# H3 convolution beside a ReLU feed-forward block: new pacing weights for the convolution's steps, and another preparation of the first two token blocks

## The chip, the cores and the metric

The kernel runs on one core of a Trainium2 chip. Its time is the device time of one execution in microseconds (us); three runs of the kernel before took 1110.46, 1113.22 and 1113.85 us, so their median is 1113.22 us. Engines are named TensorE (PE in the rows of the profile; its weight loads are PEld), VectorE (DVE), ScalarE (ACT), GpSimd (POOL) and SyncE (SP, which here only issues DMAs).

## The reference

For 2048 tokens of 576 numbers, with a hidden width of 4608:

```python
x = A_q
xn = _layernorm(x, axis=-1)                      # (x - mean) / sqrt(var + 1e-5)
return x + _A_ref(xn, A_k, A_v, A_shift_k, A_ssm_k, A_ssm_D) + _B_ref(xn, B_w1, B_w2)

# _B_ref: the feed-forward block
h = jnp.maximum(xn @ w1, 0); return h @ w2       # 576 -> 4608 -> 576

# _A_ref: k through a causal convolution of 4 taps, times v, then a causal
# convolution as long as the sequence (FFT of length 4096), a skip term, times q
k_shift = sum(k_pad[:, t:t + S] * shift_k[:, ks - 1 - t] for t in range(4))
kv = k_shift * v
y = irfft(rfft(kv, 4096) * rfft(ssm_k, 4096))[:2048] + kv * ssm_D
return q * y                                     # q is xn
```

## The kernel before, in words

**Two programs in one.** TensorE works through the feed-forward block, and the steps of the convolution are slipped in between. The 2048 tokens are four blocks of 512. A half (two blocks) is taken through all 18 groups of 256 hidden columns, then the other half; one group for one half is called a quad here, so there are 36 quads, numbered `g`. `classical` forms hidden sums with plain products in quads 0 and 1 (`PLAIN = 2`). From quad 2 on `quad` forms the two blocks' hidden sums with seven products instead of eight, on operands that are parts of the transposed tokens ("00", "01", "11") and their sums and differences ("s1" to "s4"). Every operand is held as a rounded part and the rest of it (`hi`, `lo`), so that one product of a 128-row chunk is three matmuls of 512 columns. `hidden` (L511) turns a finished PSUM bank into the operands of the second layer: ScalarE writes `hh`, then VectorE writes `ll` (L516). Two PSUM banks (pool `ps_h`) hold the hidden sums, so TensorE can start a new sum in a bank only when that bank's `ll` has been written. The second layer takes 12 matmuls of 288 columns for 128 tokens (`mm2`, tile `pso`, two tiles of two banks), which VectorE adds to `acc` (L652, L648); such a unit of 128 tokens is done eight times a quad. GpSimd forms the low parts of the weights (L439) and issues their DMAs.

**The first stage** (L1019 to L1078, pool `fa`) gets the half's operands ready. `first_xT` subtracts the mean from the tokens of block 0, transposes them on TensorE (tiles `psx`, `psf`), and splits the result; VectorE and ScalarE share the centring. The factor 1/std is left to the sums: `mm2` multiplies by `rstd` for block 0. For block 1 `second_rows` waits for statistics of all eight tiles, normalizes in full on ScalarE, and `second_xT` transposes through the two `psf` banks. From quad 1's classical sums on, `whole` puts the operands of both blocks together again from their two parts (GpSimd), `scales` makes a row of 1/std with one matmul of a diagonal matrix, `scaled` multiplies block 0 by it, and `combine`/`split_operand` make "s1" to "s4".

**The convolution** is a generator, `conv`, whose stages are: fb (`later_operands`: the second half's tokens are normalized, written to memory, read back transposed and split), fk (the filter's first transform, tiles `ks`, `wk`), fx (taps, gate, split and first transform of k and v; VectorE lines L772, L775, L776, L781 and L672; matmuls `psf<-xs,wx`), fm (the middle transforms) and fo (the way out). In fm, `spectrum` is a turn of 8 matmuls from `ztk` into two banks `psf`, copied out by four ScalarE copies (L856); `product_of` is a turn of 8 from `ztx` into the next two `psf`, multiplied out by VectorE (L871); `way_back` is a turn of 16. The pool `ps_f` has two banks in all, so each turn needs both banks of the turn before it to be read out. The matmuls of fm and fo stand in the program's order among those of the feed-forward block (`in_turn`).

**What paces it.** After each group of feed-forward matmuls `tick` adds their columns to a clock. When the convolution's clock allows, the next piece of `conv` is written into the program. A piece costs the weight that it yields (`W_FB`, `W_FK`, `W_FX`, `W_FMK`, `W_FMX`, `W_FMB`, `W_FO`); `rate` is the sum of all weights (`FFT_TOTAL`) over the columns of the feed-forward block (`SHARE` of them, less `PAUSES` times 16000 for the pauses). So only the ratios of the weights matter: they say how many feed-forward columns lie beside each stage. `here()` keeps a piece's VectorE and ScalarE instructions behind the last `acc` and the last `hh` at that place; within that, a scheduler places instructions.

Of the kernel before, what the change touches and what calls it, by code (L numbers as in the profile page):

```python
# [50 lines left out]
PAUSES = 18  # L51
SHARE = 0.993
# [53 lines left out]
def h3_ffn_kernel(ctx: ExitStack, tc, x, k, v, shift_k, ssm_k, ssm_D, w1, w2, fwd, inv, mid, out):  # L106
# [86 lines left out]
    lows = []  # L193

# [52 lines left out]
    def first_xT(pool):  # L247

        xn = rows_tiles(pool, 0)
        wide = [ps_o.tile([P, 2, 512], F32, tag="o", name=f"psx{k}") for k in range(2)]  # L250
        ps = [wide[c // 2][:, c % 2, :] for c in range(4)] + [fft_psum()]
        last = {}
        for t in range(BT):
            last[t] = centre(xn[t], acc[t], t, ("dve", "act")[t % 2], last.get(t - 2))
            transposes(ps, xn[t], t)
            keep_warm(WARM_TILE[t])
        for o in ("00", "01"):
            operand(o)
        rest_operand(0)
        with tc.issue_after(last[BT - 1].ins):  # L260
            split_a(0)
            for c in range(4):
                split_chunk(xo["00" if c < 2 else "01"], c % 2, ps[c])
            high, done["low"] = split_rest(hl[0], ps[4])
        with tc.issue_after(high.ins):
            split_r(0)
            split_b(0)
            split_d(0)
            xf["r"] = pool.tile([64, 512], F32, tag="xfr", name="xfr")
            nc.scalar.activation(xf["r"], ps[4][:64], AF.Copy)  # L270
        with tc.issue_after(done["low"].ins):
            for t in (1, 3):
                stats(t, acc[t])

    def second_rows(pool):
        xn = rows_tiles(pool, 1)
        for o in ("10", "11"):
            operand(o, "s4" if o == "10" else None)
        rest_operand(1)
        for t in range(BT, 2 * BT):  # L280
            with tc.issue_after(lows[(t - BT) // 2].ins):
                stats(t, acc[t])
        with tc.issue_after(lows[1].ins):
            last = inv_std(0, 2 * BT)
        neg = xp.tile([P, BT], F32, tag="negs", name="negs")
        with tc.issue_after(last.ins):
            nc.vector.scalar_tensor_tensor(neg, mv[:, BT:2 * BT, 0], -1.0, rstd[:, BT:2 * BT],
                                           op0=OP.mult, op1=OP.mult)
        for i in range(BT):
            t = BT + i  # L290
            nc.scalar.activation(xn[i], acc[t], AF.Identity, bias=neg[:, i:i + 1],
                                 scale=rstd[:, t:t + 1])
        return xn

    def second_xT(xn):
        for c in range(5):
            w = min(P, D - c * P)
            ps = fft_psum()
            for i in range(BT):
                nc.tensor.transpose(ps[:w, i * P:(i + 1) * P], xn[i][:, c * P:c * P + w], ident)  # L300
            if c == 4:
                split_rest(hl[1], ps)
            else:
                split_chunk(xo["10" if c < 2 else "11"], c % 2, ps)

    def whole(pool, o):

        xf[o] = pool.tile([P, 2, 512], F32, tag=f"xf{o}", name=f"xf{o}")
# [4 lines left out]
    def scales(pool):  # L313

        diag = pool.tile([P, BT, P], F32, tag="diag", name="diag")
# [798 lines left out]
```

## Time and profile before

| | |
|---|---|
| Median of three runs | 1113.22 us (1110.46 to 1113.85) |
| The profiled execution | 1111.22 us, of which its span is 1109.0 us |
| TensorE matmuls, busy | 1057.7 us, 95% of the span |
| VectorE, ScalarE, GpSimd, busy | 766.8, 478.0, 470.1 us |
| Mean granted TensorE clock | 0.981 |

Rows of the profile read: start in us from the span's begin, length in us, engine, line, operation, out<-in, shapes, count; in brackets the engine's idle time before it and what ended it. Matmuls overlap (a row's length of one is longer than the distance to the next), so a busy TensorE can still be late: pace is read from distances between starts. The stages of the profiled execution lie at about 0 to 80 us (first stage), 80 to 140 (first part of fb), 140 to 260 (rest of fb and loads), 260 to 410 (fk), 410 to 680 (fx), 690 to 970 (fm), 970 to 1109 (fo and the end).

### The profile page before, as it was taken

The page shows a single profiled execution, that of the slowest core. Times are in us where ns is not written, and L with a number is a line of the kernel's source. Part 1 is how long each engine was busy: PE and PEld are TensorE (multiplying, and loading weights), DVE is VectorE, ACT ScalarE, POOL GpSimd, SP SyncE. Part 2 cuts the span into 40 slices and gives each one's busy share as a digit, 9 for nine tenths or more (in the row PEclk, how much of TensorE's full clock was granted, in tenths as well). Part 3 has the DMA queues.
Part 4 walks back from the last instruction along what each step waited for, and adds up shares of the span by engine and source line. Part 5 has one row for each costly group of instructions (what it writes and reads, how often), then busy time and mean ns, then how long its engine had stood idle before and what let it go on. Part 6 is the DMA issues. An engine that isn't in the chain of part 4 may idle for free.

```text
span 1109.0 us, 17042 instructions
## 1 busy us (share of the span) xinstructions
PE 1057.7 (95%) x6298; PEld 876.2 (79%) x6298; DVE 766.8 (69%) x1136; ACT 478.0 (43%) x914; POOL 470.1 (42%) x504
## 2 busy tenths in 40 slices
PE   6898999999999997999999898999999999999998
PEld 3687889988999986888888787866666676788877
DVE  3888787457877757999999997444554455456665
ACT  3343344235877742443544443344444444322220
POOL 4453355344444444444444443524232423254541
PEclk8999999999999998999999998999999999999999
DMA  5144854942444447459964332386556654376754
GB/s 141 35 115 141 170 198 177 205 88 76 149 139 138 138 137 175 129 181 365 271 168 131 120 118 84 132 237 187 186 174 195 198 183 136 125 235 183 209 185 118
DMA packets 118431, 179.45 MB, mean 162 GB/s; under 512 B 66381, under 2 KB 67551, under 8 KB 116556
## 3 DMA queue, kind: packets, MB, share of 16 engines
q1 hardware_dynamic: 99212, 121.99, 37.0%
q0 software_dynamic: 18816, 55.49, 16.9%
q10 hardware_dynamic: 320, 0.88, 0.3%
q8 instruction: 50, 0.82, 0.3%
q14 instruction: 33, 0.27, 0.1%
HBM read 123.27 MB, written 45.61 MB: 152 GB/s over the span
## 4 chain that ended last, share of the span: by engine, by line
PE 67%; DVE 19%; issue 5%; DMA 4%; ACT 2%; SPq 1%; POOL 1%; DVEq 0%; POOLq 0%; ACTq 0%
PE pso L495 29%; PE psh L495 26%; PE psf L690 8%; DVE e L775 4%; DVE acc L652 3%; DVE c L776 3%; DVE ll L516 2%; PE psh_c L495 2%; PE psf L678 2%; DMA r<-in_w 1%; DVE xs L672 1%; DVE c L772 1%; DVE c L781 1%; SPq L372 1%; DVE sums L451 1%
## 5 line engine op out<-in xcount | busy, mean ns | idle before, releaser
L495 PE MATMUL pso<-w,hh 128*128 128x288 f32 x2304 | 474.5, 298 | 3.2 <-DVE acc L652 1.6
L495 PEld LDWEIGHTS pso<-w,hh 128*128 128x128 f32 x2304 | 382.5, 189 | 37.1 <-issue 9.0
L495 PE MATMUL pso<-w,ll 128*128 128x288 f32 x1152 | 340.7, 296 | 0.2 <-DVE ll L516 0.2
L652 DVE TENSOR_TENSOR acc<-pso,acc 128x576 f32<-128x576 f32 x280 | 210.7, 753 | 173.7 <-PE pso L495 172.6
L495 PEld LDWEIGHTS pso<-w,ll 128*128 128x128 f32 x1152 | 218.0, 189 | 0.4 <-DVE ll L516 0.4
L439 POOL TENSOR_TENSOR w<-r,w 128x576 fp32r<-128x576 f32 x72 | 110.6, 1542 | 139.9 <-ACT w L438 139.9
L439 POOL TENSOR_TENSOR wb<-sums,wb 128x512 fp32r<-128x512 f32 x34 | 48.1, 1414 | 205.5 <-ACT wb L438 188.8
L495 PE MATMUL psh<-x,wa 128*128 128x512 f32 x408 | 110.2, 404 | 10.1 <-DVE p L607 4.9
L495 PE MATMUL psh<-xs,wb 128*128 128x512 f32 x408 | 109.4, 400 | 1.9 <-ACT u L577 1.9
L495 PEld LDWEIGHTS psh<-x,wa 128*128 128x128 f32 x408 | 74.2, 190 | 34.2 <-issue 6.9
L495 PEld LDWEIGHTS psh<-xs,wb 128*128 128x128 f32 x408 | 71.9, 188 | 26.2 <-issue 12.4
L495 PE MATMUL psh<-hl,wr 128*128 128x512 f32 x272 | 88.2, 402 | 2.1 <-ACT psh L600 2.0
L600 ACT ACTIVATE psh<-psh 128x512 f32<-128x512 f32 x34 | 19.9, 585 | 150.8 <-DVE u L598 150.8
L516 DVE SCALAR_TENSOR_TENSOR ll<-psh,hh 128x512 fp32r<-128x512 f32 x68 | 46.7, 687 | 50.5 <-ACT hh L515 50.1
L515 ACT ACTIVATE hh<-psh 128x512 fp32r<-128x512 f32 x68 | 40.6, 597 | 84.7 <-PE psh L495 84.5
L495 PE MATMUL psh<-xs,wc 128*128 128x512 f32 x204 | 59.3, 428 | 15.4 <-DVE ll L516 15.4
L439 POOL TENSOR_TENSOR wd<-r,wd 128x256 fp32r<-128x256 f32 x36 | 34.6, 961 | 89.9 <-ACT wd L438 89.8
L439 POOL TENSOR_TENSOR wa<-r,wa 128x512 fp32r<-128x512 f32 x36 | 52.3, 1452 | 40.8 <-ACT wa L438 40.5
L672 DVE TENSOR_TENSOR ks<-kt,ks 64x288 fp32r<-64x288 f32 x64 | 54.5, 852 | 18.4 <-ACT ks L671 16.9
L495 PEld LDWEIGHTS psh<-xs,wc 128*128 128x128 f32 x204 | 40.2, 202 | 29.0 <-DVE ll L516 17.6
L495 PEld LDWEIGHTS psh<-hl,wr 128*128 128x128 f32 x272 | 47.6, 189 | 15.7 <-issue 6.6
L776 DVE TENSOR_TENSOR c<-c,e 128x576 f32<-128x576 f32 x48 | 55.3, 1152 | 0.5
(152 smaller groups left out, 1610.5 us busy)
## 6 DMA issues: line engine op xcount, KB each, us to landing
r<-in_w POOLq DMA_DIRECT2D x70, 288.0 KB, 3.5
r<-in_w POOLq DMA_DIRECT2D x35, 512.0 KB, 5.3
zk<-zk SPq DMA_DIRECT2D x32, 288.0 KB, 3.0
zx<-zx SPq DMA_DIRECT2D x32, 288.0 KB, 2.6
ztk<-zk SPq DMA_DIRECT2D x18, 512.0 KB, 3.9
ztx<-zx SPq DMA_DIRECT2D x18, 512.0 KB, 4.3
k<-k SPq DMA_DIRECT2D x72, 128.0 KB, 3.7
zy<-vo SPq DMA_DIRECT2D x18, 512.0 KB, 2.7
```

The lines of the kernel that those rows point to most:

```text
L372: nc.sync.dma_start(w[32 * i:32 * i + 32].rearrange("p (g d) -> p g d", d=32), src[:, :, d:d + 32])
L439: nc.gpsimd.tensor_tensor(w[:, 1, :n], src, w[:, 0, :n], OP.subtract)
L495: last = nc.tensor.matmul(ps, a, m, start=start and n == 0, stop=n == len(seq) - 1, skip_group_check=True)
L515: done["act"] = nc.scalar.activation(hh, ps, AF.Relu)
L516: low = nc.vector.scalar_tensor_tensor(ll, ps, 0.0, hh, op0=OP.max, op1=OP.subtract)
L600: nc.scalar.activation(x, y, AF.Copy, scale=-1.0)
L652: done["acc"] = nc.vector.tensor_tensor(two(acc[t]), ps[:, :, :NH], two(acc[t]), OP.add)
L672: nc.vector.tensor_tensor(dst[other], src[own], dst[own], OP.subtract)
L678: nc.tensor.matmul(ps[:, :NH], w[:, u, n, :], stk, start=n == 0, stop=n == 1)
L690: done["pe"] = nc.tensor.matmul(ps, a, m, start=start, stop=stop)
L775: nc.vector.tensor_tensor(e, win[t - n], sk[:, n, :], OP.mult)
L776: nc.vector.tensor_tensor(sums[t], sums[t], e, OP.add)
```

## The change

**Pacing.** All weights are new, and with them `SHARE` (0.993 to 0.99), `PAUSES` (18 to 19), `N_FB` (36 to 37) and one pause ahead of fx (1.5 to 2.5 times 16000). The sum of the weights goes from 514.4 to 971.9. Worked out from the constants, and counted in the order of the program on TensorE:

| stage | sum of weights, before and now | share of the clock, in thousand columns | columns between its first and last matmul |
|---|---|---|---|
| fb | 57.6, 144.3 | 171, 223 | none on TensorE |
| fk | 96.0, 160.0 | 284, 247 | 272192, 272192 |
| fx | 166.4, 371.2 | 493, 574 | 439008, 492256 |
| fm | 122.4, 190.8 | 362, 295 | 355712, 290304 |
| fo | 72.0, 105.6 | 213, 163 | 197376, 149760 |

**The first stage.** `block_xT` now treats both blocks alike: centred only, by VectorE and ScalarE in turn, transposed through `psx` and `psf`, split, and copied whole to `xf` by ScalarE from PSUM. `second_rows`, `second_xT` and `whole` go. All eight units of quads 0 and 1 multiply by `rstd` (L652 of the new code). `scales` and `scaled` are done for both blocks, and all of "00", "01", "11" and the rest rows are made again scaled. Each piece is now held behind the last `acc` and `hh` (`here()`), so they stand in the order in which the code is written. The weights' split of quad 0's second layer comes after block 1's centring, the DMA of its weights ahead of the last two tiles of tokens, and quad 0's units after both blocks' hidden sums. Statistics of the second half are inverted four tiles at a time (before two).

```diff
-PAUSES = 18
-SHARE = 0.993
+PAUSES = 19
+SHARE = 0.99
-W_FK, W_FX, W_FMK, W_FMX, W_FMB, W_FO = 1.5, 2.6, 1.6, 3.2, 2.0, 4.5
+W_FK, W_FX, W_FMK, W_FMX, W_FMB, W_FO = 2.5, 5.8, 2.4, 4.8, 3.4, 6.6
-N_FB, W_FB = 36, 1.6
+N_FB, W_FB = 37, 3.9
+    def block_xT(pool, b, names, tags):
...
+        for t in range(BT):
+            last[t] = centre(xn[t], acc[b * BT + t], b * BT + t, ("dve", "act")[t % 2],
+                             done["copied"] if b and t == 1 else last[t - 2])
...
+            for c in range(4):
+                nc.scalar.activation(dst[c][:, 0], ps[c], AF.Copy)
+            high = nc.scalar.activation(hl[b][:64], ps[4][:64], AF.Copy)
+            for c in range(4):
+                nc.vector.tensor_tensor(dst[c][:, 1], ps[c], dst[c][:, 0], OP.subtract)
...
+            for o, src in zip(names, wide):
+                xf[o] = pool.tile([P, 2, 512], F32, tag=f"xf{o}", name=f"xf{o}")
+                nc.scalar.activation(xf[o], src, AF.Copy)
...
-    def whole(pool, o):
...
-            nc.gpsimd.tensor_tensor(xf[o][:, c, :], xo[o][:, 0, c, :].bitcast(F32),
-                                    xo[o][:, 1, c, :].bitcast(F32), OP.add)
...
-        if g < PLAIN and b == 0:
+        if g < PLAIN:
...
-            yield -1.5 * PAUSE
+            yield -2.5 * PAUSE
...
     with tc.tile_pool(name="fa", bufs=1) as fa:
-        first_xT(fa)
-        load_w1(1)
+        block_xT(fa, 0, ("00", "01"), (None, None))
         classical(0, 0, 0, 1, 1)
         classical(0, 0, 1, 0, 2)
-        xn = second_rows(fa)
+        block_xT(fa, 1, ("10", "11"), ("s4", None))
+        load_w1(1)
+        with tc.issue_after(done["low"].ins):
+            inv_std(0, 2 * BT)
         for j in range(FT):
             split_w2(0, j)
             load_w2(1, j)
-        for i in range(BT):
-            open_unit(0, 0, i)
-            mm2(0, 0, i)
-        second_xT(xn)
         classical(0, 1, 0, 1, 0)
...
+        for i in range(BT):
+            unit(0, i)
+        row = scales(fa, 0)
+        scaled(row, "00", "01", 0)
         classical(1, 0, 0, 0, 0)
-        row = scales(fa)
-        for o in ("00", "01"):
-            whole(fa, o)
         unit(1, 0)
         unit(1, 1)
...
+        row = scales(fa, 1)
+        scaled(row, "11", "10")
+        combined(fa, "s1")
+        made("s1")
         classical(1, 0, 1, 1, 0)
...
         unit(1, 2)
         unit(1, 3)
-        sums(2)
...
+        combined(fa, "s2")
+        made("00")
+        made("01")
+        made_rest(0)
+        made("s2")
         classical(1, 1, 0, 0, 0)
         split_a(2)
+        sums(2)
```

**The order at three places.** On ScalarE at the very start, before (`wa0`, `wr0`, `wb0`, `wd0` are first-layer weights, `w20` second-layer weights, `x00`, `x01`, `hl0` the operands of block 0, `psx` and `psf` the transposed tokens):

```order
L438 ACTIVATE wa0_205<-r1_0_106 128x512
L208 ACTIVATE x00_202<-psx0_155 128x512
L208 ACTIVATE x01_203<-psx1_156 128x512
L438 ACTIVATE w20_313<-r2_0_0_117 128x576
L204 ACTIVATE hl0_204<-psf_157 64x512
L438 ACTIVATE wr0_218<-r1_0_106 128x256
L438 ACTIVATE wb0_221<-r1_0_106 128x256
L438 ACTIVATE wd0_224<-r1_0_106 128x256
L438 ACTIVATE w20_318<-r2_0_1_119 128x576
L208 ACTIVATE x00_202<-psx0_155 128x512
L208 ACTIVATE x01_203<-psx1_156 128x512
```

and now:

```order
L444 ACTIVATE wa0_205<-r1_0_106 128x512
L274 ACTIVATE x00_202<-psx00_155 128x512 x2
L274 ACTIVATE x01_203<-psx01_156 128x512 x2
L275 ACTIVATE hl0_204<-psf_157 64x512
L444 ACTIVATE wr0_218<-r1_0_106 128x256
L444 ACTIVATE wb0_221<-r1_0_106 128x256
L444 ACTIVATE wd0_224<-r1_0_106 128x256
L286 ACTIVATE xf00_227<-psx00_155 128x1024
L286 ACTIVATE xf01_229<-psx01_156 128x1024
```

The split of the second-layer weights `w20` no longer stands between the four copies of block 0's operands; it now follows the centring of block 1.

On VectorE in the middle of fx, from a quad's first `acc` on, before (`c`, `e` are the taps, `xs` the split for the transform, `ll` and `acc` belong to the feed-forward block):

```order
L652 TENSOR_TENSOR acc0_100<-pso16_0_5047,acc0_100 128x576
L772 TENSOR_TENSOR c5_5078<-k5_5016,sk_4180 128x576
L781 TENSOR_TENSOR c4_4891<-c4_4891,v4_4828 128x576
L652 TENSOR_TENSOR acc0_100<-pso16_1_5064,acc0_100 128x576
L775 TENSOR_TENSOR e5_1_5103<-k4_4825,sk_4180 128x576
L672 TENSOR_TENSOR xs4_0_5036<-c4_4891,xs4_0_5036 64x576
L672 TENSOR_TENSOR xs4_1_5058<-c4_4891,xs4_1_5058 64x576
L776 TENSOR_TENSOR c5_5078<-c5_5078,e5_1_5103 128x576
L516 SCALAR_TENSOR_TENSOR ll17_0_0_5117<-psh17_1_5045,hh17_0_0_5116 128x512
L652 TENSOR_TENSOR acc2_103<-pso16_2_5083,acc2_103 128x576
```

and now:

```order
L656 TENSOR_TENSOR acc8_5371<-pso19_8_5922,acc8_5371 128x576
L769 TENSOR_TENSOR c8_5944<-k8_5854,sk_4258 128x576
L656 TENSOR_TENSOR acc8_5371<-pso19_9_5930,acc8_5371 128x576
L772 TENSOR_TENSOR e8_1_5969<-k7_5667,sk_4258 128x576
L773 TENSOR_TENSOR c8_5944<-c8_5944,e8_1_5969 128x576
L522 SCALAR_TENSOR_TENSOR ll20_0_0_5981<-psh20_1_5920,hh20_0_0_5980 128x512
L656 TENSOR_TENSOR acc10_5465<-pso19_10_5949,acc10_5465 128x576
```

Ahead of the same third `acc` there are six of the convolution's instructions before and three now. Over the stage, VectorE's order holds 69 `acc` between the first tap and the last split before, and 77 now.

On TensorE in fm, between the turns of one `spectrum` (`ztk9`) and the next `product_of` (`ztx8`), before:

```order
L690 MATMUL psf_8437<-ztk9_8194,m_sb_7271 64x512 x2
L690 MATMUL psf_8438<-ztk9_8194,m_sb_7271 64x512 x2
L495 MATMUL psh27_4_8356<-x11_5351,wc27_8161 128x512 x6
L495 MATMUL psh27_4_8356<-hl3_5355,wr27_8079 128x512 x2
L495 MATMUL psh28_1_8467<-x00_5061,wa28_8270 128x512 x3
L690 MATMUL psf_8473<-ztx8_8214,m_sb_7271 64x512 x2
L690 MATMUL psf_8474<-ztx8_8214,m_sb_7271 64x512 x2
```

and now:

```order
L687 MATMUL psf_8803<-ztk9_8583,m_sb_7771 64x512 x2
L687 MATMUL psf_8804<-ztk9_8583,m_sb_7771 64x512 x2
L501 MATMUL psh29_2_8640<-xs3_5161,wb29_8550 128x512 x3
L687 MATMUL psf_8824<-ztx8_8625,m_sb_7771 64x512 x2
L687 MATMUL psf_8825<-ztx8_8625,m_sb_7771 64x512 x2
```

Eleven feed-forward matmuls lie between the two turns before and three now. Over the 17 pairs of such turns the mean distance is 5052 feed-forward columns before and 3290 now (from 3072 to 7552, and from 1536 to 4992).

More of the change, by code (lines that the diff above doesn't have):

```diff
@@ L272, in first_xT @@
             for t in (1, 3):
[L273 to L288, printed above, removed]
-        for i in range(BT):
[L290 to L293, printed above, removed]
@@ L313, in scales @@
[L313 to L329 removed]
+                stats(b * BT + t, acc[b * BT + t])
```

156 lines of the change are left out of this document (80 added, 76 removed).

## The prediction

> **What bounds the kernel now.** I read the stages first: the stretches of the span (us; then busy time and count of PE, PEld, DVE, ACT, POOL; granted clock; DMA share; GB/s).
>
> ```profile
> 0.00:80.00 80.00, 65.61 (x321) 50.86 (x322) 51.05 (x87) 33.88 (x59) 39.37 (x44) 0.91 0.36 92
> 80.00:140.00 60.00, 54.21 (x305) 47.39 (x304) 47.19 (x101) 19.77 (x41) 24.30 (x25) 0.97 0.63 156
> 140.00:260.00 120.00, 119.38 (x714) 107.99 (x713) 75.12 (x114) 45.24 (x84) 59.67 (x62) 1.00 0.60 160
> 260.00:410.00 150.00, 149.49 (x917) 136.57 (x916) 116.14 (x164) 110.75 (x209) 70.83 (x79) 1.00 0.41 134
> 410.00:680.00 270.00, 245.21 (x1407) 217.33 (x1406) 254.71 (x320) 112.78 (x227) 122.35 (x124) 0.96 0.59 180
> 680.00:970.00 290.00, 290.00 (x1822) 205.28 (x1822) 140.52 (x227) 123.22 (x236) 93.33 (x101) 1.00 0.55 169
> ```
>
> TensorE never waits in the rest of fb, in fk and in fm. It waits in the first stage, in the first part of fb, and in fx (410 to 680), where VectorE is busy 254.7 of 270 us and TensorE gets through least. The changed weights give fx more feed-forward work to hide behind and fm less, so the question is what a quad costs each engine there. Without a convolution a quad is 24.6 us, from the chain of waits, the same place in two successive quads:
>
> ```profile
> 146.66 1.85 PE psh L495 x8
> ...
> 171.26 1.85 PE psh L495 x8
> ```
>
> That is 24.6 / 53248 = 0.462 ns a column. In fx, the timeline of TensorE at one stall, and then that of VectorE up to it:
>
> ```profile
> 500.42 2.93 PE L495 MATMUL psh<-xs,wc 128*128 128x512 f32 x6 [2.34 <-DVE ll L516]
> ```
>
> ```profile
> 496.27 1.54 DVE L672 TENSOR_TENSOR xs<-c,xs 64x576 fp32r<-64x576 f32 x2
> 497.83 1.93 DVE L776 TENSOR_TENSOR c<-c,e 128x576 f32<-128x576 f32 x1
> 499.69 0.68 DVE L516 SCALAR_TENSOR_TENSOR ll<-psh,hh 128x512 fp32r<-128x512 f32 x1
> 500.95 0.74 DVE L775 TENSOR_TENSOR e<-k,sk 128x576 f32<-128x576 f32 x1
> ```
>
> `ll`, which frees the bank, stands behind the convolution's splits and taps. VectorE's queue, not one instruction, is the bound.
>
> **The sum.** It is made against the profiled execution, 1111.22 us with a span of 1109.0; the median of the runs, 1113.22, is 2.0 above it, and I add that at the end.
>
> *fx.* Its window from the first tap to the last split, and VectorE's groups in it:
>
> ```profile
> 421.00:679.00 258.00, 235.28 (x1350) 208.80 (x1351) 250.84 (x314) 110.52 (x223) 119.98 (x121) 0.96 0.58 181
> L776 DVE TENSOR_TENSOR c<-c,e 128x576 f32<-128x576 f32 x48 | 55.3, 1152 | 0.5
> L652 DVE TENSOR_TENSOR acc<-pso,acc 128x576 f32<-128x576 f32 x69 | 51.7, 749 | 3.7 <-PE pso L495 3.5
> L775 DVE TENSOR_TENSOR e<-k,sk 128x576 f32<-128x576 f32 x42 | 45.1, 1075 | 0.2
> L516 DVE SCALAR_TENSOR_TENSOR ll<-psh,hh 128x512 fp32r<-128x512 f32 x18 | 12.2, 680 | 0.2
> L516 DVE SCALAR_TENSOR_TENSOR ll<-p,hh 128x512 fp32r<-128x512 f32 x9 | 10.4, 1154 | 0.0
> L516 DVE SCALAR_TENSOR_TENSOR ll<-u,hh 128x512 fp32r<-128x512 f32 x9 | 8.4, 933 | 0.0
> L451 DVE TENSOR_TENSOR sums<-r 128x256 f32<-128x256 f32 x16 | 7.1, 486 | 0.0
> L451 DVE TENSOR_TENSOR sums<-sums,r 128x256 f32<-128x256 f32 x16 | 6.7, 418 | 0.1
> L607 DVE TENSOR_TENSOR p<-psh,p 128x512 f32<-128x512 f32 x9 | 6.1, 681 | 0.1
> L598 DVE TENSOR_TENSOR u<-psh,u 128x512 f32<-128x512 f32 x8 | 5.5, 686 | 0.1
> ```
>
> 69 `acc` are 8.6 quads: TensorE alone would need 8.6 x 24.6, and 128 transform matmuls of 288 columns at 0.462 ns a column (17.0), together 229 us. The window is 258, so 29 us go to VectorE. The order now holds 77 `acc`, one quad more. A quad adds to VectorE 8 x 0.749 + 2 x 0.680 + 1.154 + 0.933 + 2 x 0.486 + 2 x 0.418 + 0.681 + 0.686 = 12.6 us; the convolution's own instructions are as many as before. So VectorE needs 250.8 + 12.6 = 263.4, with the 7.2 it idled before 270.6; TensorE alone 229 + 24.6 = 253.6. Lost: 17, a gain of 12. Against that, taps of the same form take 0.74 us in the timeline and 1.075 and 1.152 in the mean, 34 us more over L775 and L776, while GpSimd works. If that lengthening goes with GpSimd's work, which is the same in every quad, and not with the number of taps, one quad more costs 34 / 8.6 = 4 us more, and the gain is 8. I take 10. The bounds: 6, if VectorE also idles more as its queue thins; 14, if its queue empties in the later quads, where the order has 15 of the convolution's instructions a quad and had 16 to 20. The first two quads of fx are as dense as before (20 and 23 to a quad, 21 and 21 before), so the stage does not become free.
>
> The Trainium skill ("SBUF — State Buffer", section "SBUF: two separate sides") says that a VectorE instruction with two SBUF inputs and a GpSimd instruction that reads SBUF take a shared pair of ports in turn, each for its whole length. By that the lengthening goes with GpSimd's work, and the sum would take 8 for fx; the long taps agree with it, but no row here tells it from a cost by tap.
>
> *fk.* The columns between its first and last matmul are the same to the last, and TensorE was busy 149.5 of 150 us: nothing.
>
> *fm.* Here the change costs. TensorE's timeline of a second turn of a pair that lies far apart, then of a pair that lies close, and below it ScalarE's timeline between the two turns of that close pair:
>
> ```profile
> 761.12 1.09 PE L690 MATMUL psf<-ztx,m_sb 64*64 64x512 f32 x8
> ...
> 841.19 1.09 PE L690 MATMUL psf<-ztk,m_sb 64*64 64x512 f32 x8
> 842.21 1.66 PE L495 MATMUL psh<-xs,wb 128*128 128x512 f32 x6
> 843.80 1.71 PE L690 MATMUL psf<-ztx,m_sb 64*64 64x512 f32 x8
> ```
>
> ```profile
> 842.32 2.06 ACT L856 ACTIVATE k<-psf 128x512 f32<-128x512 f32 x4 [0.35 <-PE psf L690]
> ```
>
> The `ztk` turn ends at 842.28; ScalarE's four copies read its two banks until 844.38; the `ztx` turn starts 1.52 us after the end, with 3072 columns between, and lasts 0.62 longer than a free one. So a turn needs 2.14 us, or 4400 columns, behind the one before; each column that is missing costs 0.462 ns. Of the 17 distances now, three are 3456, six 3072, two 2560, two 1536, the rest above: missing 20200 columns, 9.3 us. Before: two of 3072, one of 3456, one of 4096, 3900 columns, 1.8 us. So fm costs 7.5 us. Bounds: 4, if copies come before a turn's end, and 11, if other ScalarE work stands ahead of them. The other turns keep 2560 columns behind two copies, which is enough (two of four copies take 1.0 us), and 6016 or more behind VectorE's four products.
>
> *fo.* Its turns lie 7552 columns or more apart (3.5 us), with two VectorE instructions to free the banks: nothing.
>
> *The first stage.* There the timelines of ScalarE, of TensorE, and of VectorE:
>
> ```profile
> 17.20 0.68 ACT L438 ACTIVATE w<-r 128x576 fp32r<-128x576 f32 x1 [4.48 <-DMA r<-in_w]
> ```
>
> ```profile
> 20.39 0.80 PE L495 MATMUL psh_c<-x,wa 128*128 128x512 f32 x1 [6.87 <-ACT x L208]
> 21.37 3.78 PE L495 MATMUL psh_c<-x,wa 128*128 128x512 f32 x8 [0.18 <-DVE x L209]
> 52.13 4.54 PE L495 MATMUL psh_c<-x,wa 128*128 128x512 f32 x12 [3.07 <-DVE ll L516]
> 73.00 1.53 PE L495 MATMUL psh<-x,wa 128*128 128x512 f32 x6
> ```
>
> ```profile
> 35.40 0.87 DVE L317 TENSOR_SCALAR diag<-ident,rstd 128x128 f32<-128x128 f32 x4
> 46.66 3.60 DVE L329 TENSOR_TENSOR xf<-xf,row 128x512 f32<-128x512 f32 x4
> ```
>
> ScalarE stood still for a weight's DMA ahead of block 0's copies. Now they come first, so TensorE's wait of 6.9 us goes, with 1.7 for eight matmuls that ran at half pace behind it. VectorE gives most of it back. Between block 0's last `acc` in quad 0 and the `ll` that frees the bank of quad 2's first product its order now has two diagonals (1.7), ten scalings (9.0 at 0.9; 6.8 at the 0.68 of L607), three `ll` (2.0), four `acc` (3.2), six differences, nine splits and two sums (11.6 at 0.68): 27 us, 25 at the least. TensorE waits twice for a diagonal behind its own last unit (0.8 + 0.9 each). I put that `acc` at 39 us: block 0's sums end 8.6 us before the 29.3 of this trace, then come, as estimates at 0.462 ns a column, 20 transposes and their copies (4.8), 28 matmuls (6.6), four units (6.4) and the `acc` (0.8). Then quad 2 starts at 66 to 69 instead of 73.0, 4 to 7 gained. Some twelve more VectorE instructions (8.2 us) than before stand ahead of its first `acc`; I leave 2. Bounds: -3, if all of those are waited for, and +7.
>
> *fb.* A wait of VectorE and SyncE's issues, in their timelines, and TensorE's two longest waits:
>
> ```profile
> 119.40 0.71 DVE L382 STREAM_TRANSPOSE yf<-xw 128x512 f32<-128x512 f32 x1 [3.02 <-DMA xw<-rows_n]
> ```
>
> ```profile
> 113.26 18.49 SPq L372 DMA_DIRECT2D xw<-rows_n  x28
> ```
>
> ```profile
> 86.93 1.43 PE L495 MATMUL psh<-xs,wb 128*128 128x512 f32 x5 [1.38 <-ACT u L577]
> 134.01 2.00 PE L495 MATMUL psh<-x,wa 128*128 128x512 f32 x6 [2.33 <-ACT psh L562]
> ```
>
> A step's four DMAs take SyncE 4 x 0.66 = 2.6 us. A step had 1.6 x 2962 = 4739 columns (2.2 us) and has 3.9 x 1545 = 6027 (2.8), so the loads keep up. Of the 5.8 us that TensorE idled from 80 to 140 I take 3.5; bounds 0 and 6.
>
> Sum: 1111.2 - 10 (fx) + 7.5 (fm) - 2 (first stage) - 3.5 (fb) = 1103.2, or 1105 against the median.
>
> **The rivals.** *Slower: the short waits of fm cool TensorE's clock.* Behind the 2.34 us gap at 500.42 six matmuls took 2.93 us against 1.66 at 842.21, 1.3 lost beside the wait. The turn at 843.80, with waits under half a us, was followed by no slow matmuls, which speaks against it. If waits as short as 0.4 to 1.4 us, 13 of them within 130 us, do it, each costs 1.3 more, 17 us: 1122. It decides from about eight such turns on. The Trainium skill ("TensorE: Matmul & The Clock Gate", "A second HAM failure mode: psum-queue depth-cycling") describes such a case: brief idling between groups of matmuls as PSUM banks are cycled, and a clock that swings. By that rule this rival would hold; fm's granted clock of 1.00 is no sign of it so far.
>
> *The same: fx returns less.* VectorE stays the bound at the lower end (6), the first stage returns nothing, fm costs 8: 1113.2 - 6 - 2 + 8 = 1113. For it speaks that 263 us of VectorE still exceed TensorE's 254.
>
> *Better: VectorE's queue empties.* fx 14, first stage 6, fb 5, fm 6: 1094. For it speaks the count of 15 a quad.
>
> **How the numbers follow.** About 0.3%, 3.3 us, is what a measurement of this kernel tells from no change. Forecast, 1099 to 1109.9: 0.50. Better: 0.20. The same, to 1116.5: 0.18. Slower: 0.12. So faster 0.70. The range leaves out the lower part of the better case and most of the slower: 1096 to 1115.
>
> **What would show it.** Right: fx holds a quad more at 27 to 28.5 us a quad (30 now); `psf<-ztx` turns last 1.5 us or more where 3072 columns or fewer lie between; no wait of ScalarE for a weight before the first `hh`, but TensorE waiting for `diag`; fewer waits on `xw`. Wrong: TensorE as idle in fx as before, matmuls at half pace in fm, or quad 2 starting after 73 us.

## The result, and the profile after

The changed kernel takes 1096.9 us (median of four runs, 1095.74 to 1097.91), the kernel before 1111.84 (four runs, 1109.77 to 1113.85). The ratio is 0.9865, with a 95% interval of 0.9841 to 0.9889: about 15 us less. The forecast was 1105, which is 8.2 less than the 1113.22 it was made against and 6.8 less than 1111.84: the direction was right and the time lies inside the range, but the gain is about twice the one forecast. The profiled execution took 1097.09 us with a span of 1095.0, so 14.0 of span are to be explained.

The stages of the changed kernel first (the columns are those of the same view of before: stretch, length, busy time and count of PE, PEld, DVE, ACT, POOL, granted clock, DMA share, GB/s):

```profile
0.00:80.00 80.00, 66.22 (x335) 51.31 (x336) 58.93 (x112) 41.70 (x78) 29.75 (x37) 0.96 0.31 82
80.00:140.00 60.00, 54.23 (x316) 47.50 (x315) 43.20 (x89) 18.62 (x36) 27.18 (x29) 1.00 0.72 168
282.00:424.00 142.00, 141.46 (x872) 129.59 (x872) 110.52 (x153) 106.77 (x203) 70.00 (x79) 1.00 0.42 135
437.00:704.60 267.60, 253.04 (x1510) 229.19 (x1511) 260.39 (x332) 120.15 (x239) 132.61 (x133) 0.99 0.58 178
743.00:970.40 227.40, 224.16 (x1375) 139.99 (x1374) 104.79 (x170) 98.90 (x189) 64.35 (x69) 0.99 0.62 188
```

The fourth row is fx from its first tap to its last split, 437.0 to 704.6. In the 258.0 us of the same stretch TensorE did 1350 matmuls before; now it does 1510 in 267.6. The fifth row is fm: TensorE, which was busy in every microsecond there, now stands for 3.2 us.

A busy TensorE can be late, since a matmul's row is longer than the distance to the next. So from here on TensorE's loss is counted by distances: every matmul is charged the distance that its form keeps where nothing waits (0.2315 us for 512 columns, 0.1328 for 288, 0.117 for those of fm, about 0.07 for those of fo, which start in pairs), and what a stretch lasts beyond that sum is lost. An example: of fx's 1350 matmuls before 924 had 288 columns and 426 had 512, so 924 x 0.1328 + 426 x 0.2315 = 221.3 us of work in 258.0 us, 36.7 lost; now 1034 and 476, 247.5 us in 267.6, 20.1 lost. By stage, with two of the kernels of the next section:

| lost by TensorE, us | before | changed | new pacing alone | new first stage alone | forecast of the difference |
|---|---|---|---|---|---|
| start to fk's first matmul | 36.1 | 29.9 | 33.6 | 32.0 | -5.5 (first stage -2, fb -3.5) |
| fk | 1.5 | 1.1 | 1.6 | 1.2 | 0 |
| fk's last matmul to fx's first tap | 2.4 | 0.1 | 0.0 | 2.0 | none made |
| first tap to fx's last matmul | 38.0 | 20.3 | 20.5 | 38.8 | -10 |
| fm | 14.9 | 27.1 | 24.9 | 18.3 | +7.5 |
| fo and all the rest | 18.1 | 17.9 | 18.4 | 17.8 | 0 |
| sum | 111.0 | 96.4 | 99.0 | 110.1 | -8 |

Two terms are off: fx gives 20 us with its entry, not 10, and fm costs 12.2, not 7.5. The other rows came out within 1 us, the first of them only as a sum: its two parts, first stage and fb, were each off by 1 to 2 us in opposite directions (4.1 and 2.5 us won where each was changed alone, 2 and 3.5 forecast).

The loss in fx is of two kinds. From fk's last matmul to fx's last, before and then in the changed kernel:

```profile
406.14:690.71 284.57, 259.78 (x1496) 230.93 (x1495) 262.15 (x334) 116.38 (x235) 123.09 (x125) 0.96 0.57 175
```

```profile
424.39:713.35 288.96, 274.27 (x1642) 248.40 (x1641) 271.40 (x352) 125.25 (x250) 135.72 (x137) 0.99 0.59 177
```

TensorE stood for 24.8 us of the 40.4 lost before (38.0 and 2.4 in the table), and for 14.7 of 20.4 now. The rest is matmuls that run slowly. Around some of the waits the granted clock was 0.50: before in five stretches, 23.9 us together (from 421.9, 438.9, 500.4, 558.4 and 674.5), now in two, 6.8 us together (from 440.5 and 498.5). The matmuls in these stretches took 9.3 us more than their charge before, and 3.0 now. So of the 20 us won, 10.1 are waits, 6.3 are matmuls at half the clock, and 3.6 are small delays around the waits. The whole executions say the same: the mean granted clock was 0.978 to 0.987 in the runs of before, and 0.991 or 0.992 in those of the changed kernel.

VectorE's groups in fx of the changed kernel, to be held against those of before:

```profile
L656 DVE TENSOR_TENSOR acc<-pso,acc 128x576 f32<-128x576 f32 x77 | 57.5, 748 | 2.7 <-PE pso L501 2.3
L773 DVE TENSOR_TENSOR c<-c,e 128x576 f32<-128x576 f32 x48 | 45.1, 940 | 0.5
L772 DVE TENSOR_TENSOR e<-k,sk 128x576 f32<-128x576 f32 x42 | 42.4, 1009 | 0.1
L676 DVE TENSOR_TENSOR xs<-c,xs 64x576 fp32r<-64x576 f32 x32 | 36.5, 1142 | 2.0 <-ACT xs L675 1.0
L522 DVE SCALAR_TENSOR_TENSOR ll<-p,hh 128x512 fp32r<-128x512 f32 x10 | 11.6, 1155 | 0.0
```

There are 77 `acc`, as the order said. VectorE is busy 260.4 us, 9.6 more than before; the forecast had 12.6 more, and 4 more yet if its long instructions grew in number. They did not: over all 160 instructions of the convolution (taps, gates, splits) VectorE took 160.9 us before and 158.8 now, so that the shorter taps are balanced by longer splits (1142 ns in the mean; 811 before).

TensorE in the first stage of the changed kernel:

```profile
39.09 1.12 PE L302 MATMUL psf<-diag,ones 128*128 128x512 f32 x2 [1.69 <-DVE diag L298]
48.30 1.12 PE L302 MATMUL psf<-diag,ones 128*128 128x512 f32 x2 [1.69 <-DVE diag L298]
68.80 2.90 PE L501 MATMUL psh<-x,wa 128*128 128x512 f32 x6 [6.55 <-DVE ll L522]
```

The wait of 6.9 us at 20.39 is gone. The two waits for a diagonal are there with the price that was forecast for them (0.8 + 0.9). Quad 2 starts at 68.80; the forecast was 66 to 69, and 73.0 before. TensorE stands 6.55 us ahead of it, for VectorE.

In fm, TensorE at the wait that the forecast did not have, and below it VectorE:

```profile
756.38 1.08 PE L687 MATMUL psf<-ztk,m_sb 64*64 64x512 f32 x4 [2.51 <-issue]
757.62 1.74 PE L687 MATMUL psf<-ztk,m_sb 64*64 64x512 f32 x4 [0.16 <-DVE k L868]
759.29 2.57 PE L501 MATMUL psh<-xs,wb 128*128 128x512 f32 x6
...
773.41 1.94 PE L687 MATMUL psf<-ztx,m_sb 64*64 64x512 f32 x8
```

```profile
754.94 2.54 DVE L868 TENSOR_TENSOR k<-psf,k 128x512 f32<-128x512 f32 x4 [4.93 <-DMA k<-k]
```

The row at 773.41 is the kind of wait that was forecast: a product turn 2560 columns behind a spectrum turn, spread over 1.94 us in place of 1.09. The wait at 756.38 is another. fm's first product stood in its banks from 750.2 on, but VectorE could not multiply it out until the filter's values had come back from the DMAs that swap their halves (`k<-k`), at 754.94. The third spectrum turn needs those banks: 2.51 us of standing, and then six matmuls in 2.57 us where 1.54 is usual.

### The profile page after: what moved, and what is told of

Same layout as the page of the kernel before. It is cut to its first block, busy times and chain, and to the rows that moved or that the text cites. A ratio compares the mean times of both kernels' runs of the same rounds, so it can differ in the third digit from the quotient of the medians.

```text
span 1095.0 us, 17070 instructions
## 1 busy us (share of the span) xinstructions
PE 1051.7 (96%) x6300; PEld 870.8 (80%) x6300; DVE 769.9 (70%) x1149; ACT 485.5 (44%) x929; POOL 457.8 (42%) x496
## 5 line engine op out<-in xcount | busy, mean ns | idle before, releaser
L656 DVE TENSOR_TENSOR acc<-pso,acc 128x576 f32<-128x576 f32 x272 | 204.6, 753 | 158.0 <-PE pso L501 156.7
L501 PEld LDWEIGHTS psh<-x,wa 128*128 128x128 f32 x408 | 74.7, 190 | 32.6 <-issue 12.7
L501 PEld LDWEIGHTS psh<-xs,wb 128*128 128x128 f32 x408 | 72.9, 189 | 25.0 <-issue 11.7
L521 ACT ACTIVATE hh<-psh 128x512 fp32r<-128x512 f32 x68 | 40.6, 598 | 91.0 <-PE psh L501 90.7
L445 POOL TENSOR_TENSOR wd<-r,wd 128x256 fp32r<-128x256 f32 x36 | 31.7, 881 | 97.1 <-ACT wd L444 97.1
L868 DVE TENSOR_TENSOR k<-psf,k 128x512 f32<-128x512 f32 x72 | 44.7, 682 | 36.5 <-PE psf L687 31.6
L676 DVE TENSOR_TENSOR ks<-kt,ks 64x288 fp32r<-64x288 f32 x64 | 54.5, 852 | 18.1 <-ACT ks L675 17.0
L501 PEld LDWEIGHTS psh<-hl,wr 128*128 128x128 f32 x272 | 46.9, 188 | 19.2 <-issue 12.3
L521 ACT ACTIVATE hh<-p 128x512 fp32r<-128x512 f32 x34 | 21.5, 632 | 90.4 <-DVE p L611 65.4
L501 PE MATMUL psh<-xs,wc 128*128 128x512 f32 x204 | 53.3, 396 | 8.1 <-DVE ll L522 8.1
```

Source lines behind the costliest of these rows:

```text
L445: nc.gpsimd.tensor_tensor(w[:, 1, :n], src, w[:, 0, :n], OP.subtract)
L501: last = nc.tensor.matmul(ps, a, m, start=start and n == 0, stop=n == len(seq) - 1, skip_group_check=True)
L521: done["act"] = nc.scalar.activation(hh, ps, AF.Relu)
L656: done["acc"] = nc.vector.tensor_tensor(two(acc[t]), ps[:, :, :NH], two(acc[t]), OP.add)
L676: nc.vector.tensor_tensor(dst[other], src[own], dst[own], OP.subtract)
L868: nc.vector.tensor_tensor(filt[n][c][:, k, :], banks[k], filt[n][c][:, k, :], OP.mult)
```

## The experiments

Where a kernel is compared with the changed one below, it is by their ratios to the kernel before, each measured beside it.

The theory that the prediction stood on: in fx VectorE's queue as a whole is the bound, so a quad more returns the difference between TensorE's and VectorE's work for a quad; in fm each column missing between two turns costs its time; the first stage gives little. After the result its rival: the loss lies in single dense stretches, above all at fx's entry, and is not a matter of the stage's sum.

### The two halves of the change apart

*New pacing alone:* the kernel before with

```diff
-W_FK, W_FX, W_FMK, W_FMX, W_FMB, W_FO = 1.5, 2.6, 1.6, 3.2, 2.0, 4.5
+W_FK, W_FX, W_FMK, W_FMX, W_FMB, W_FO = 2.5, 5.8, 2.4, 4.8, 3.4, 6.6
-N_FB, W_FB = 36, 1.6
+N_FB, W_FB = 37, 3.9
-            yield -1.5 * PAUSE
+            yield -2.5 * PAUSE
```

and with it `PAUSES`, `SHARE` and the statistics in fours.

> The kernel before with the new weights, the new pauses and the statistics inverted four tiles at a time; the old first stage. Its feed-forward columns between the turns of fx, fm and fo are the same to the last as in the changed kernel. As the prediction priced it (fx -10, fm +7.5, part of fb -3.5) it stands 4 to 6 us below before. If the trace of the changed kernel has it right (fx with its entry -20, fm +12), it stands 8 to 10 below, and the first stage gives the rest of the 15.

Measured: 0.9896 of before (0.9871 to 0.992), 12.8 us less by the medians (1099.48 against 1112.26). So the pacing is most of the change, and it is worth about twice what the forecast's terms for it add up to.

*New first stage alone:* the changed kernel with the old weights, `PAUSES`, `SHARE` and pause.

```diff
-W_FK, W_FX, W_FMK, W_FMX, W_FMB, W_FO = 2.5, 5.8, 2.4, 4.8, 3.4, 6.6
+W_FK, W_FX, W_FMK, W_FMX, W_FMB, W_FO = 1.5, 2.6, 1.6, 3.2, 2.0, 4.5
-N_FB, W_FB = 37, 3.9
+N_FB, W_FB = 37, 1.6
```

> The changed kernel with the old weights and pauses; only the first stage is new. The prediction's term: 2 us faster than before, bounds 3 slower and 7 faster. If the two parts only add up, the traces give about 6 faster. The rival, that the time won ahead of quad 2 is given back in quads 2 and 3, where VectorE has more to do: 0 to 2 faster.

Measured: 0.9991 (0.9971 to 1.0011), no difference that can be told. Its trace shows 4.1 us won up to fk (36.1 to 32.0 in the table) and 3.4 lost in fm, where the same weights, begun at another place of the program, put some turns closer. So the forecast of -2 is neither borne out nor refuted by the time; and the two halves add up to the whole within the intervals (0.9896 x 0.9991 = 0.9887).

### Is it the width of fx?

*fx widened alone:* the kernel before with fx given the columns of the changed kernel.

```diff
-W_FK, W_FX, W_FMK, W_FMX, W_FMB, W_FO = 1.5, 2.6, 1.6, 3.2, 2.0, 4.5
+W_FK, W_FX, W_FMK, W_FMX, W_FMB, W_FO = 1.3, 3.15, 1.6, 3.2, 2.0, 3.2
```

> The kernel before with fx given one quad more (492256 columns between its first and last transform matmul, as in the changed kernel), taken from fo (197 to 138 thousand); fm and the first stage stay as before. The prediction's term for fx: 10 us faster, bounds 6 to 14. If one quad more costs VectorE only the 10 us that its window grew by in the trace of the changed kernel: 15 to 20 faster. If fo has to pay for it: less than 10.

Measured: 0.9911 (0.989 to 0.9932), 10 us. TensorE's loss in fx behind the first tap went from 38.0 to 24.9, or by 12.3 with the piece ahead of the tap (2.4 to 3.2); fm took 3.2 back. So the quad as such was priced rightly, at the 12 of the sum and not at the 10 taken. The changed kernel, with the same 492256 columns, loses 7.7 us less than this one in fx and its entry: something else in the new numbers pays too. Of these 7.7 us, 2.9 are waits and 4.1 are matmuls at half the clock (17.1 us of it in this kernel's fx, 6.8 in the changed one's).

*fx wider by another quad:* the changed kernel with

```diff
-W_FK, W_FX, W_FMK, W_FMX, W_FMB, W_FO = 2.5, 5.8, 2.4, 4.8, 3.4, 6.6
-N_FB, W_FB = 37, 3.9
+W_FK, W_FX, W_FMK, W_FMX, W_FMB, W_FO = 2.5, 6.4, 2.4, 4.8, 3.4, 6.6
+N_FB, W_FB = 37, 3.0
```

> The changed kernel with yet one quad more for fx (545504 columns), taken from fb, so that fk and fx start a quad earlier. If VectorE's queue is still what bounds fx on the whole, another quad returns 12 to 16 us, less some 2 that a denser fb costs: 10 to 14 faster than the changed kernel. If what is left of the loss lies at the entry and in the first two dense quads, which this does not thin out: 0 to 5 faster.

Measured: 0.9936 of before (0.991 to 0.9961); the changed kernel has 0.9865, so this is some 8 us slower than it. In fx TensorE loses 19.4 behind the first tap and 1.8 ahead of it: nothing more was returned (20.4 together in the changed kernel). VectorE's busy time there, beside 290.8 us of stretch:

```profile
426.60:717.40 290.80, 277.54 (x1654) 250.59 (x1655) 277.05 (x350) 127.47 (x256) 141.93 (x142) 0.99 0.54 168
```

VectorE has 13.8 us of slack, twice that of before, and TensorE still stands. So the stage's sum does not say what is lost, and the theory falls there. What the columns cost at the other end is seen in fb: 42.4 us lost up to fk, 12.5 more than in the changed kernel. Of these, 6.5 are more standing and 5.5 are more matmuls at half the clock. The waits of TensorE there are like these:

```profile
97.80 1.22 PE L501 MATMUL psh<-hl,wr 128*128 128x512 f32 x2 [2.17 <-ACT psh L604]
...
140.77 1.95 PE L501 MATMUL psh<-xs,wc 128*128 128x512 f32 x6 [2.79 <-DVE ll L522]
```

The kernel with the new first stage alone gives fb hardly more room (175 thousand columns of the clock, 171 here) and loses 32.0; why this one loses 10 more was not followed up.

### Where in fx it is lost

Cut into stretches of half a quad (26624 columns) from fk's last matmul on, with TensorE's loss in us and, in brackets, the number of the convolution's instructions that VectorE starts in it:

| half quads | before | changed |
|---|---|---|
| 1 and 2 (first tap in 1) | 5.1 (1), 7.4 (13) | 2.9 (1), 7.0 (12) |
| 3 to 6 | 0.0 (8), 1.7 (11), 1.8 (11), 4.8 (13) | 0.0 (11), 0.0 (9), 4.3 (13), 1.1 (10) |
| 7 to 12 | 0 (6), 1.8 (10), 0 (8), 4.0 (10), 0 (8), 0.9 (8) | 0 (7), 0 (7), 1.3 (8), 0.1 (8), 0 (7), 0 (8) |
| 13 to 18 | 0.6 (8), 3.7 (10), 0 (8), 1.0 (9), 0.4 (7), 7.3 (11) | 0 (7), 2.5 (8), 0 (8), 0 (7), 0 (7), 0 (7) |
| 19 and 20 | 0 (0), 0 (0) | 0 (7), 1.8 (8) |

Before, eight half quads with ten or more instructions lose 32.5 us, and nine with six to nine lose 2.9. Now four have ten or more and lose 12.4. By this a quad more pays by what it takes out of the full stretches; the ones that are left over, at the entry, are as dense as they were.

That the count alone decides is not shown. It hangs on where the cuts lie: with every cut a quarter of a quad earlier, the seven half quads of before with ten or more lose 21.1 us, and the ten others behind the first still 11.8. And the place in the quad parts the loss as well as the count does: the even half quads of before in the table, 2 to 18, lose 32.6 us, the odd ones from 3 on 2.8. Six of TensorE's waits in fx, 15.4 of the 24.8 us, come at one place of a quad, ahead of the product `psh<-xs,wc`, for the `ll` that frees its bank. Count and place were not taken apart.

The last dense stretch of before ended in the longest of these waits, of which the changed kernel has a short one; TensorE in before, then in the changed kernel:

```profile
676.51 2.93 PE L495 MATMUL psh<-xs,wc 128*128 128x512 f32 x6 [4.19 <-DVE ll L516]
```

```profile
701.30 1.66 PE L501 MATMUL psh<-xs,wc 128*128 128x512 f32 x6 [1.39 <-DVE ll L522]
```

At the entry, VectorE of the changed kernel and then TensorE:

```profile
436.84 0.76 DVE L769 TENSOR_TENSOR c<-k,sk 128x576 f32<-128x576 f32 x1 [4.68 <-DMA k<-in_k]
```

```profile
439.52 2.14 PE L501 MATMUL psh<-x,wa 128*128 128x512 f32 x6 [2.65 <-DVE p L611]
448.99 0.53 PE L501 MATMUL pso<-w,hh 128*128 128x288 f32 x2 [1.23 <-DVE acc L656]
455.81 1.66 PE L501 MATMUL psh<-xs,wc 128*128 128x512 f32 x6 [3.57 <-DVE ll L522]
496.35 0.74 PE L501 MATMUL psh<-hl,wr 128*128 128x512 f32 x2 [1.47 <-ACT psh L604]
```

The first tap waits on VectorE for its rows of `k`, and an `ll`, an `acc` and the difference `p` that TensorE needs stand behind it. That is 2.65 us of TensorE here; it was more in before, VectorE first and then TensorE:

```profile
420.86 0.76 DVE L772 TENSOR_TENSOR c<-k,sk 128x576 f32<-128x576 f32 x1 [5.91 <-DMA k<-in_k]
```

```profile
423.54 2.93 PE L495 MATMUL psh<-x,wa 128*128 128x512 f32 x6 [4.41 <-DVE p L607]
```

*The entry thinned:* fx's steps are put into the program long before fk's matmuls are through, so those steps pile up at the entry; a longer pause spreads them. The columns come from fo.

```diff
-            yield -2.5 * PAUSE
+            yield -5.5 * PAUSE
-W_FK, W_FX, W_FMK, W_FMX, W_FMB, W_FO = 2.5, 5.8, 2.4, 4.8, 3.4, 6.6
+W_FK, W_FX, W_FMK, W_FMX, W_FMB, W_FO = 2.5, 5.8, 2.4, 4.8, 3.4, 4.6
-PAUSES = 19
+PAUSES = 22.3
```

> The changed kernel with the pause ahead of fx three longer, so that the convolution's instructions at fx's entry stand 8, 7, 13, 7, 8, 7 to four acc on VectorE in place of 7, 13, 7, 16, 6, 11; the columns come from fo (105 thousand now). If a stretch is lost by its own density, the 15 us that TensorE loses in the first two and a half quads of fx fall to about 6: 7 to 10 us faster than the changed kernel. If only the stage's mean counts, as the prediction's sum had it: fx is 44 thousand columns wider, another 12 or more. If the entry's loss is the wait for the first tap's load alone: 0 to 2 faster.

Measured: 0.9778 of before (0.9737 to 0.9819), about 9 us below the changed kernel. TensorE at the entry:

```profile
456.23 0.53 PE L501 MATMUL pso<-w,hh 128*128 128x288 f32 x2 [0.23 <-DVE acc L656]
458.44 0.73 PE L501 MATMUL psh<-hl,wr 128*128 128x512 f32 x2 [0.36 <-ACT psh L604]
470.52 0.53 PE L501 MATMUL pso<-w,hh 128*128 128x288 f32 x2 [0.63 <-DVE acc L656]
476.57 2.50 PE L501 MATMUL psh<-xs,wc 128*128 128x512 f32 x6 [2.26 <-DVE ll L522]
```

The first six half quads lose 0.1, 0, 1.4, 5.0, 0 and 0 us with 1, 6, 9, 12, 8 and 7 instructions: 6.5 in place of 15.3, as the expectation had it from the density. The later ones, with 7 and 8 in turn, lose up to 1.7 in every second one, each time ahead of `psh<-xs,wc`, although the changed kernel mostly loses nothing at such counts: here the place tells and the count does not. So fx as a whole falls only from 20.4 to 16.7, with 44 thousand columns more than in the changed kernel. The other 5 us came from fm (27.1 to 21.8), where the wait at 756.38 is not there: the later start has moved it. The expectation had no term for this, so that the total of 7 to 10 came out is in part luck.

### What lengthens the taps

*No low parts in fx:* in the changed kernel GpSimd writes zeros for the low parts of the weights of quads 16 to 26, in place of subtracting; the sums of those quads lack that term.

```diff
-        nc.gpsimd.tensor_tensor(w[:, 1, :n], src, w[:, 0, :n], OP.subtract)
+        if 16 <= g <= 26:
+            nc.gpsimd.memset(w[:, 1, :n].bitcast(F32), 0.0)
+        else:
+            nc.gpsimd.tensor_tensor(w[:, 1, :n], src, w[:, 0, :n], OP.subtract)
```

> The changed kernel without GpSimd's low parts of the weights of quads 16 to 26 (it writes zeros instead, so these products lack a term); all else stays. If VectorE's taps are lengthened by GpSimd's work, the convolution's 154 instructions in fx fall from 159 us towards 116, and fx loses 5 us or less in place of 20: 12 to 15 faster than the changed kernel. If they are lengthened by their number or by transfers: no change beyond 2 us.

Measured: 0.9725 (0.9691 to 0.9759), 14 to 16 us below the changed kernel. The stretch of fx, VectorE's groups in it, and one of GpSimd's:

```profile
437.00:694.80 257.80, 253.83 (x1530) 230.87 (x1531) 216.75 (x333) 120.11 (x239) 68.64 (x132) 0.99 0.61 186
```

```profile
L776 DVE TENSOR_TENSOR c<-c,e 128x576 f32<-128x576 f32 x48 | 36.1, 753 | 0.5
L775 DVE TENSOR_TENSOR e<-k,sk 128x576 f32<-128x576 f32 x42 | 31.5, 750 | 0.2
L679 DVE TENSOR_TENSOR xs<-c,xs 64x576 fp32r<-64x576 f32 x32 | 24.1, 753 | 1.8 <-ACT xs L678 0.8
L525 DVE SCALAR_TENSOR_TENSOR ll<-p,hh 128x512 fp32r<-128x512 f32 x10 | 6.8, 684 | 0.0
```

```profile
L446 POOL MEMSET w<- 128x576 f32 x20 | 11.6, 581 | 45.5 <-PE pso L504 45.5
```

Every form is back at its short time, to the last instruction: the 160 take 120.3 us, not 158.8, and not one is over 0.9 us. VectorE is busy 217 us, and fx with its entry loses 10.4 in place of 20.4. The rest of the gain is fm's first wait, absent here too. So GpSimd's subtractions lengthen VectorE's instructions, by 38.5 us over 69 of them, 0.56 each. Over all traces of fx in which GpSimd subtracts it is 0.54 to 0.66 for each. Among the lengthened are only those with both inputs in SBUF (`ll<-p,hh`, 1155 to 684 ns); `acc<-pso,acc` and `ll<-psh,hh`, with one input in PSUM, took 748 and 681 all along. By the Trainium skill ("SBUF — State Buffer", section "SBUF: two separate sides") such an instruction and a GpSimd instruction that reads SBUF hold a shared pair of ports in turn, each for its whole length; these rows agree with it. Not every such instruction was lengthened, though: `sums<-r`, which reads SBUF alone, took 416 ns in the changed kernel and 418 here.

### fm's two costs

*A hold ahead of fm's first product:* the changed kernel with

```diff
+                    if n == 0:
+                        yield -PAUSE / 2
                     product_of(n)
```

> The changed kernel with 8000 columns more between the second spectrum turn of fm and its first product. If TensorE's 2.5 us stand there and the slow matmuls behind it come from the product's wait for its data's second half, they go: 4 to 5 us faster than the changed kernel. If the DMAs are simply slow there whatever stands behind: 0 to 1.

Measured: 0.9827 (0.9791 to 0.9863), about 4 us below the changed kernel (0.9865); the intervals of the two overlap, so the trace has to tell. TensorE at the same turns, then VectorE's product:

```profile
755.93 1.09 PE L687 MATMUL psf<-ztx,m_sb 64*64 64x512 f32 x8
760.12 1.09 PE L687 MATMUL psf<-ztk,m_sb 64*64 64x512 f32 x8
762.38 2.06 PE L687 MATMUL psf<-ztx,m_sb 64*64 64x512 f32 x8 [0.29 <-ACT k L853]
```

```profile
757.05 2.48 DVE L868 TENSOR_TENSOR k<-psf,k 128x512 f32<-128x512 f32 x4 [1.64 <-PE psf L687]
```

The product now waits for its turn and not for a DMA, and the spectrum turn at 760.12 finds its banks free. fm's loss fell from 27.1 to 22.1, by the 5.0 us of that wait and the slow matmuls behind it.

*fm's columns shared out anew:* the changed kernel with

```diff
-W_FK, W_FX, W_FMK, W_FMX, W_FMB, W_FO = 2.5, 5.8, 2.4, 4.8, 3.4, 6.6
+W_FK, W_FX, W_FMK, W_FMX, W_FMB, W_FO = 2.5, 5.8, 3.2, 4.2, 3.2, 6.6
```

> The changed kernel with fm's columns shared out otherwise: 3.2, 4.2, 3.2 in place of 2.4, 4.8, 3.4, so that the mean distance from a spectrum turn to a product turn is 5391 columns (3290 before). By the prediction's price for a missing column, 7 us of fm's cost go, less 1 to 2 where copies now stand short behind a product: 4 to 7 faster than the changed kernel. If the short distances cost nothing, or the product turns take it back: 0 to 2.

Measured: 0.9819 (0.9784 to 0.9854), 4 to 5 us below the changed kernel, again with intervals that overlap. The 17 product turns cost TensorE 12.9 us in the changed kernel, 6.8 here and 6.2 in before (waiting ahead of them, stretching within them, and slow matmuls behind them); the turns of the way back cost 2.9 more, since they now stand shorter behind a product. The wait at fm's start is 2.5 us shorter, not gone. The price by missing columns holds.

### A version that beats both

Three kernels on top of the thinned entry (pause of 5.5, `PAUSES` of 22.3): with the hold and other shares for fm; with a smaller change of the shares and no hold; and with the hold and fo cut to 81 thousand columns. Their weights in that order:

```diff
-W_FK, W_FX, W_FMK, W_FMX, W_FMB, W_FO = 2.5, 5.8, 2.4, 4.8, 3.4, 4.6
+W_FK, W_FX, W_FMK, W_FMX, W_FMB, W_FO = 2.5, 5.8, 3.2, 4.2, 3.2, 4.6
+W_FK, W_FX, W_FMK, W_FMX, W_FMB, W_FO = 2.5, 5.8, 3.0, 4.4, 3.2, 4.6
+W_FK, W_FX, W_FMK, W_FMX, W_FMB, W_FO = 2.5, 6.1, 3.0, 4.4, 3.2, 3.4
```

> The thinned entry together with fm's columns shared out anew (mean distance 5602) and the hold ahead of fm's first product. If the parts add up: fm loses 18 us in place of the 22 of the kernel with the thinned entry alone, which stood 25 below before, so 27 to 30 below before. If fm's turns only trade one wait for another: 24 to 26 below.

> The thinned entry with a smaller change of fm's shares (3.0, 4.4, 3.2; mean distance 4841) and no hold. By the price of the missing columns 2 to 3 us less than the kernel with the thinned entry alone; if the wait at fm's start comes back, 2 to 3 more than it.

> As the first of these, with fo down to 81 thousand columns and fx and fm a little wider. If fo's loss of 11.5 us is the pace of its own matmuls, whatever feed-forward work lies between them, as it was the same at 150 and 105 thousand columns: 0 to 3 us below the first. If fo's loads come late at last: 3 or more above it.

Measured: 0.9732 (0.9705 to 0.976), 0.975 (0.9728 to 0.9772) and 0.9775 (0.9749 to 0.9801). The first stands at 1083.44 us against 1114.49 of before beside it, some 14 below the changed kernel, and its fm loses 15.9 us where the changed kernel loses 27.1. The third failed what was expected of it: fo's loss, which was 11.5 to 11.7 at 150 and at 105 thousand columns, is 16.7 at 81, so fo has a floor of its own between these.

## Why the prediction was right or wrong

**fx, the step that failed.** The term for fx was mis-sized: it was put at 10 us and is 20 with the entry, of which 10.1 are waits and 6.3 matmuls at half the clock. Three things in its working failed. First, TensorE's own work was taken as 69 `acc` at 24.6 us a quad, 229 us with the transforms; counted by matmuls it is 221. The matmuls of the first two of the 69 `acc` lie ahead of the stretch (they end at 417.27, the first tap starts at 420.86), eight of the 128 transform matmuls lie behind it, and the 24.6 us hold 0.3 more than a quad's matmuls need (96 x 0.1328 + 50 x 0.2315 = 24.3). So 36.7 us were lost there, not 29, and there was more to win. Secondly, the 12 of the sum was cut to 10, in case the lengthening by GpSimd came once more with the added quad. It was 40.6 us before and 38.5 in the changed kernel: its cause was the one that the prediction suspected, but it did not grow, although GpSimd's subtractions in fx went from 62 to 69. Why it did not is open. Thirdly, and most, the loss was treated as one sum over the stage. It lies in single places, most of it in the half quads with ten and more of the convolution's instructions, or in one place of the quad that falls into them; and the matmuls at half the clock around some of the waits cost again. The prediction saw 1.3 us of these behind one wait, but had no term for them in fx. It also had the counts, 20 and 23 in the first two quads and 15 in the later ones, and used them only for a bound. The widening alone gave 12.3 in fx; of the other 7.7, which came with where the new numbers put the instructions, 3.1 lie in the first half quad (6.0 us in the kernel with fx widened alone, 2.9 in the changed one) and 3.9 in the half quads with ten and more (four in each of the two, 16.3 and 12.4 us). How much of this is the new place of the first tap within its quad, and how much the weights, was not taken apart.

**fm, the second.** The close turns cost 6.7 us more than before, 7.5 forecast; the price by missing columns was right. The other 5.0 are one wait, at fm's first product. The sentence "6016 or more behind VectorE's four products" being enough was wrong there: it counted VectorE's work and left out the DMAs on which that work waits at the start, when the swaps of two spectra come at once.

**The first stage and fb.** Forecast -5.5, measured -6.2 together. The causes named for the first stage are there: ScalarE's wait gone, two diagonals at 1.69 us, quad 2 at 68.8 us. But the two terms were not right one by one: run alone, the first stage won 4.1 us up to fk, not 2, and the pacing 2.5, not 3.5, so that the sum came out near is in part luck. Of the 6.2, only 1.2 are shorter standing (20.8 to 19.6 us); 4.4 are matmuls that no longer ran at half the clock (at 0.50 for 17.1 us up to fk before, for 6.8 now). In the time of the whole kernel the gain of the first stage alone cannot be told from none (0.9991).

**fk and fo at nothing.** Right: -0.4 and -0.2.

**The rivals.** That short waits in fm cool TensorE's clock did not happen: the turns that waited under 0.5 us are followed by matmuls at their usual pace, and the granted clock there is 0.99. Only the one wait of 2.51 us had slow ones behind it, with the granted clock at 0.50 for 3.4 us. The swinging clock that the Trainium skill describes ("TensorE: Matmul & The Clock Gate", "A second HAM failure mode: psum-queue depth-cycling") is not seen in fm of this trace. Of the rival in which VectorE's queue empties, fx came true beyond its price (14), the rest not.

## What to carry to other kernels

A stage that is bound by an engine's queue loses time in single places, where the other engine needs a buffer back and the queue is full, so cost it piece by piece (here by half quads) and not by the stage's busy time. Look at where in the repeating work the waits stand as well as at how full the pieces are, since a table of pieces changes with its cuts. Price the slow matmuls behind a wait with the wait. When work is given more room, look first at the densest piece: another quad of room returned nothing more here, and spreading the entry took its loss from 15.3 to 6.5 us. When a step is drawn closer to the one before, ask of every input of the waiting instruction when it arrives, those that come by DMA too.

## What the runs showed of the hardware that was not expected

GpSimd's subtractions cost VectorE 0.54 to 0.66 us each, 37 to 47 us over fx in every trace that has them, although the two engines work on different data there.

The slow matmuls behind a wait of TensorE go with the granted clock, and not with the length of the wait alone: six took 2.50 us behind a wait of 2.26 (thinned entry, at 476.57), but 1.66 behind one of 3.57 (changed kernel, at 455.81). The stretches behind these two waits; the granted clock is the third number from the end:

```profile
477.10:480.50 3.40, 3.40 (x12) 2.98 (x11) 3.30 (x5) 1.23 (x2) 1.46 (x1) 0.50 1.00 381
```

```profile
455.81:459.22 3.41, 3.41 (x20) 3.11 (x21) 3.32 (x5) 0.60 (x1) 0.00 (x0) 1.00 0.54 182
```

In fx of the two main traces the clock fell to a half for 3.4 us or twice that at a time. What brings it down behind one wait and not behind another is not shown by these runs.
